# Clustered order for all of batch 2, and batch 3's fetches behind the last block

## The chip, the core and the metric

One NeuronCore of a Trainium2 chip runs the whole program. The time is the device time of one execution in microseconds (us). Five engines work side by side, each in the order of its own queue, and wait for each other by semaphores: TensorE (PE, matmuls; its weight loads are listed as PEld), VectorE (DVE), ScalarE (ACT), GpSimd (POOL), and SyncE (SP), which here only issues DMAs. PE writes to PSUM, the others read it from there.

## The reference

Clustered attention, then a two-layer network, in float32. Every query and key belongs to the cluster whose centroid is nearest in direction, and a query attends to the keys of its own cluster only.

```python
batch, n_heads, seq, head_dim, n_clusters = 4, 8, 768, 64, 16
q_assign = argmax(einsum('bhsd,hcd->bhsc', q_n, c_n))       # k_assign likewise
mask = q_assign[:, :, :, None] == k_assign[:, :, None, :]
scores = where(mask, scale * q @ k.T, -1e9)
attn = softmax(scores) @ v                                   # (4, 8, 768, 64)
x = attn.transpose(0, 2, 1, 3).reshape(3072, 512)
h = x @ w_in                                                 # (3072, 2048)
out = (maximum(h, 0) + alpha * minimum(h, 0)) @ w_out        # (3072, 512)
```

## The kernel before

**Pairs, units, steps.** Work on attention goes by pairs of heads: `pairs` has 16 of them, number n = 4 * batch + pair. A *dense* pair is computed in two halves of 384 queries, each against all six chunks of 128 keys, with everything outside the cluster multiplied by zero (`mask`, L806). A *clustered* pair (n >= `NO` = 10, so 10 and 11 of batch 2 and all of batch 3) has its rows sorted by cluster first; then each chunk of keys needs only the queries of its neighbouring chunks (`window`), 16 blocks of 128 x 128 instead of 36. One half of a dense pair, or one clustered pair, is a unit of three steps u; from step 24 (`TOGETHER`) a unit has 15 ticks: three in which it scores (`score`, L765) and weighs the unit before (`weigh`, `weigh_near`), and twelve slots.

**Filler.** PE's other work is the network on half a batch (`ffn_pieces`): 16 hidden pieces (L1027) and 12 final pieces (L1045), 28 in all. `feeds` says at which step the pieces of which half batch become available, `begun_at` where blocks of steps begin, and the slots of a block take its pieces evenly, down to `kept` pieces that stay for the next. Blocks after step 48 are 48 to 60 (pairs 10, 11, first halves of 8 and 9; pieces of the second half of batch 1), 60 to 66 (second halves of 8 and 9; batch 2, first half) and 66 to 78 (pairs 12 to 15; batch 2, second half). Behind step 78 (`NS`) come the 12 pieces kept, and then `last_pieces`: the network on batch 3 in a form with fewer products (L1205, L1261). `w_in_sums` prepares `w_in` for it and is tied to two of the last kept pieces.

**Sorting a pair.** `ORDERS` gives the step at which a clustered pair's q and k are loaded. `order_features` (DVE transposes) and `order_sims` (PE) follow, then a chain on DVE (`order_counts` to `order_clusters`: argmax, a scan, ranks, the clusters of the sorted places), spread over ticks. `order_rows` then puts the pair's 24 scatters and six stage loads into the deque `sorting`. `order_stage` loads four blocks of rows of q, k and v by three DMAs on SP's queue into one of two stages; `order_scatter` (L663, POOL) writes one block to its sorted places in DRAM by an indirect DMA. In each slot of the main loop the deque is emptied up to one scatter, so 12 a unit. `order_load`, 3 or 4 steps before the pair's first step, reads the sorted rows back (12 DMAs on SP).

**Back to the rows.** In the unit after a clustered pair, `normalise_near` (DVE) writes its outcome, `to_rows` (L964, PE, and a copy on ACT, L967) turns it, and `put_back` (L972, POOL) writes it to its rows by 12 indirect DMAs, one a tick from 8 and from 14 ticks behind `normalise_near`. `fetch_back` (L984) reads it again by four DMAs on SP's queue, 20 ticks behind `normalise_near`, and nine ticks later `turn_back` (L991, DVE) transposes it into `xT`, the network's input. For the last pair these distances are shorter (`dense`).

**Rows sums.** `total` (L856) sums the softmax denominators on PE in the last slot of a unit; `invert` (L869) takes their reciprocals on DVE a few ticks later. `misc()` is a single PSUM buffer that `total`, the second side of `weigh_near`, `to_rows`, `order_sims` and others share in turn.

Of the kernel before, what the change touches and what calls it, by code (L numbers as in the profile page):

```python
# [23 lines left out]
def kernel(  # L24
# [70 lines left out]
    def later(slots, piece):  # L95
        due.setdefault(now[0] + slots, []).append(piece)
# [5 lines left out]


    pairs = [(b, hp) for b in range(B) for hp in range(NCH)]
    NO = WHOLE * NCH - 2
    NP = len(pairs)
    raw_qk, vts = {}, {}

# [383 lines left out]
    def second_part():  # L492

        first_part.close()
        for name, bufs in (("emore", 1), ("ordc", 1), ("ordp", 1), ("order", NP - NO),
                           ("xmore", 1), ("byrow", 1)):
# [148 lines left out]
    def order_stage(n, i):  # L645
# [5 lines left out]
        for src, p0, d0 in ((q, 0, 0), (k, TS, 0), (v, TS, D)):  # L651
            nc.sync.dma_start(out=t[p0:p0 + TS, :, d0:d0 + D],
                              in_=src[b, head, rows].rearrange("(x p) d -> p x d", p=TS))

    def order_scatter(n, i, x):
        h, part = divmod(i, PARTS)
        m = NX // PARTS
        xx = part * m + x
        if x == 0:
            nc.gpsimd.tensor_copy(  # L660
                out=sorts["stage"][i % STAGES].bitcast(I32)[0:TS, :, D],
                in_=sorts["number"][0:TS, part * m:(part + 1) * m])
        nc.gpsimd.indirect_dma_start(  # L663
            out=scratch[n][1][h * NX + xx],
            out_offset=bass.IndirectOffsetOnAxis(ap=ranks[n][:, xx, h:h + 1], axis=0),
            in_=sorts["stage"][i % STAGES][:, x, :], in_offset=None,
            element_offset=h * 2 * S * P)

    def order_load(n):
        whole = scratch.pop(n)[0]  # L670
        found = sorts["order"].tile([P, 2, NJ, 1], I32, name="found")
        for h in range(2):
            r0 = 2 * h * S
            nc.sync.dma_start(out=found[:, h], in_=whole.bitcast(I32)[
                r0:r0 + S, D:D + 1].rearrange("(j p) d -> p j d", p=P))
        orders[n] = found
        for w in range(2):
            raw = inp.tile([P, 2, NJ, D], FP32, name="qk")
            for h in range(2):
                r0 = (2 * h + w) * S  # L680
                for x in range(D // Q):
                    r = h * D + x * Q
# [32 lines left out]
    for b in range(B):  # L715
        whole = [n for n in range(b * NCH, (b + 1) * NCH) if n >= NO]
        rest = [n for n in range(b * NCH, (b + 1) * NCH) if n < NO]
        begun_at.append(len(steps))
        steps += [(n, None, s) for n in whole for s in range(SB)]
        for half in range(2) if rest else ():  # L720
            if half:
                begun_at.append(len(steps))
            steps += [(n, half, s) for n in rest for s in range(SB)]
            feeds[len(steps)] = b, half
    begun_at.append(len(steps))
    assert NJ == 6 and GROUP == 2

# [209 lines left out]
    def normalise_near(n):  # L937
        outT = inp.tile([P, 2, NJ, D], FP32, name="qk").rearrange("p h j d -> p (h j d)")
        for side in range(2):
            nc.vector.tensor_tensor(out=outT[:, side * HS:(side + 1) * HS],  # L940
                                    in0=pos.pop((n, side))[:, 0:HS],
                                    in1=rds.pop((n, side)), op=ALU.mult)
        whole = tc.dram_tile([2 * S, D], FP32, name=f"back{n}")
        to = dram_disjoint_views(whole, 2 * NJ)
        found = orders.pop(n)
        place = found[:, :, :, 0]
        nc.vector.tensor_scalar(out=place, in0=place, scalar1=0, scalar2=S - 1,
                                op0=ALU.max, op1=ALU.min)
        rows = [sorts["byrow"].tile([P, HJ, P], FP32, name=f"rows{i}") for i in range(2)]

        dense = n == NP - 1
        starts = (6, 9) if dense else (6, 12)
        for i in range(2):
            later(starts[i], lambda i=i: to_rows(outT, rows, i))
            for x in range(NJ):
                later(starts[i] + 2 + (x // 2 if dense else x),
                      lambda i=i, x=x: put_back(to, place, rows, i * NJ + x))
        later(starts[1] + 2 + (HJ if dense else NJ), lambda: fetch_back(n, whole))

    def to_rows(outT, rows, i):  # L960

# [12 lines left out]
            out_offset=bass.IndirectOffsetOnAxis(ap=place[:, h, j:j + 1], axis=0),  # L974
            in_=rows[j // HJ][:, j % HJ, h * D:(h + 1) * D], in_offset=None, element_offset=h * S * D)

    def fetch_back(n, whole):

        b, hp = pairs[n]
        raw = inp.tile([P, 2, NJ, D], FP32, name="qk").rearrange("p h j d -> p (h j d)")  # L980
        for h in range(2):
            for x in range(D // Q):
                r = h * D + x * Q
                nc.sync.dma_start(  # L984
                    out=raw[r:r + Q, :].rearrange("p (t i) -> p t i", i=Q),
                    in_=whole[h * S:(h + 1) * S, x * Q:(x + 1) * Q].rearrange(
                        "(t p) i -> p t i", p=Q))

        def turn_back():
            for half in range(2):  # L990
                nc.vector.transpose(out=x_tile(b, half)[:, hp, :],  # L991
                                    in_=raw[:, half * HS:(half + 1) * HS])
        later(4 if n == NP - 1 else 9, turn_back)

    def x_tile(b, half):
        if (b, half) not in xTs:
# [330 lines left out]
    FREE = SLOTS * SB - 3  # L1327


    ORDERS = [26, 30, 34, 38, 41, 51]  # L1330
    prep_at, load_at = {}, {}
    for (n, half), u in start_of.items():
        def at(step, slot, piece):
            prep_at.setdefault((step, slot), []).append(piece)
        if half is None:
            t = ORDERS[n - NO]
            load_at.setdefault(t, []).append(lambda n=n: load(n))
            for i in range(2):
                at(t + 2, 2 + i, lambda n=n, i=i: order_features(n, i))
            at(t + 3, FIRST + 1, lambda n=n: order_sims(n))  # L1340
            load_at.setdefault(u - (3 if n == NO + 1 else 4), []).append(
                lambda n=n: order_load(n))
            at(u - 4, 0, lambda n=n: prep_clusters(n))
            for i in range(2):
                at(u - 1, i, lambda n=n, i=i: order_blocks(n, i))
                at(u - 1, FIRST + i, lambda n=n, i=i: order_queries(n, i))
            continue
# [39 lines left out]
    def feed_block(u):  # L1387
        if u == NS:

            for i, p in ((5, 0), (7, 1)):  # L1390
                ffn[i] = lambda piece=ffn[i], p=p: (piece(), w_in_sums(p))
            ffn.extend(last_pieces())
            return
        ffn.extend(ffn_pieces(*feeds[u]))

    def kept(u):


        return {NS: 12, begun_at[-2]: 8, begun_at[-3]: 2}.get(block_end(u), 0)

    def block_end(u):
        return min(x for x in begun_at if x > u)
# [59 lines left out]
    for u in range(TOGETHER, NS + 1):  # L1462
# [4 lines left out]
        if s == 0 or u == NS:  # L1467
# [2 lines left out]
            tick()  # L1470
            if u < NS:
                score(n, half, range(0, NJ // 2), alone=NJ // 2 - 1)
            tick()
            if prior[1] is None:
                invert(prior[0], 0, 1)
# [22 lines left out]
            if half is None:  # L1498
# [2 lines left out]
                         lambda n=n: (turn(n, 0), rows_sums(n, 0)),  # L1501
                         lambda n=n, E=of: add_near(n, 1, E),
                         lambda n=n: (turn(n, 1), rows_sums(n, 1))]
                todo += [lambda: None] * 4 + [lambda n=n: total(n)]
            else:
                todo.append(lambda E=E: add_up(E[1], E[0]))
                for c in range(2, NJ):
                    todo.append(lambda c=c, E=E: add_up(E[c]))
                todo.append(lambda n=n, half=half: (turn(n, half), rows_sums(n, half)))
                todo += [lambda: None] * 2  # L1510
                todo.append(lambda n=n: total(n))
            slots = range(3, SLOTS)
        else:
            slots = range(SLOTS)
# [2 lines left out]
        for i in slots:  # L1517
# [4 lines left out]
            room = (block_end(u) - block_start(u)) // SB * FREE  # L1522
            pieces = len(ffn) - kept(u) + -whole * (room - 1 - at_slot) // room
            todo.popleft()()
            while sorting:
                scatters, piece = sorting.popleft()
                piece()
                if scatters:
                    break
            feed(max(pieces, 0))  # L1530
            if (s, i) == (SB - 1, SLOTS - 1) and unfinished[0]:
                feed(1)
# [225 lines left out]
```

## Time and profile before

| | |
|---|---|
| median of 4 runs (lowest, highest) | 989.3 us (984.01, 997.01) |
| profiled execution, its own time | 989.48 us |
| its span, first to last instruction | 987.4 us |
| mean granted TensorE clock | 0.986 |
| DMA traffic | 73.35 MB, mean 74 GB/s |
| scatters, L663 on POOL | 144, 157.8 us busy, mean 1095 ns |
| put-backs, L972 on POOL | 72, 76.0 us busy, mean 1056 ns |

The units' first scores stand in PE's timeline at these times (us): step 48 at 454.0, 51 at 479.4, 54 at 525.6, 57 at 563.4, 60 at 594.2, 63 at 639.1, 66 at 682.8, 69 at 710.1, 72 at 736.9, 75 at 765.3; step 78 begins at 791.5, `last_pieces` at 834.75. Busy times in some of these stretches, in us (in brackets the instructions), then the granted clock, the DMA share and GB/s; the columns are the stretch, its length, PE, PEld, DVE, ACT, POOL:

```profile
421.10:454.00 32.90, 32.58 (x117) 15.18 (x116) 26.30 (x45) 5.75 (x11) 10.32 (x12) 1.00 0.31 74
454.00:479.40 25.40, 25.40 (x111) 13.54 (x110) 22.84 (x43) 6.88 (x14) 6.07 (x7) 1.00 0.95 135
479.40:525.60 46.20, 40.52 (x141) 18.79 (x140) 29.04 (x55) 7.75 (x16) 27.76 (x31) 0.93 0.29 66
525.60:563.40 37.80, 25.77 (x115) 13.70 (x114) 20.80 (x36) 7.77 (x15) 16.58 (x17) 0.82 0.17 41
```

How to read the other views: "x4 ... <- ..." is a group of instructions with what it writes and reads; "[0.30 <-issue]" is the idle time of the engine just before and what ended it ("issue": nothing that the profile shows); in a list of waits the three numbers are the total in us, how often, and the longest. In the row of slices each digit is a busy share in tenths of a fortieth of the span, 24.7 us.

### The profile page before, as it was taken

Reading aid. Unit: us, or ns where it says so; the run is one execution under the profiler, and the core shown is the slowest. Engines: PE = TensorE matmul, PEld = TensorE weight load, DVE = VectorE, ACT = ScalarE, POOL = GpSimd, SP = SyncE. Lnnn points to the kernel's source line nnn. Section 1 sums busy time; section 2 is a strip of 40 time slices with the busy share of each in tenths; the row PEclk is TensorE's granted clock in tenths of the full one; section 3 lists DMA queues with packets and bytes.
Section 4 is the critical chain, followed back from the end, with each engine's and each line's share of the span. In section 5 each row is a group of like instructions: output and inputs, shape, how many; then the busy total and the mean of one; then the engine's idle time right before and its main releaser. Section 6 shows DMA issues by size and latency. Waiting matters only on the chain.

```text
span 987.4 us, 11347 instructions
## 1 busy us (share of the span) xinstructions
PE 940.6 (95%) x3995; PEld 502.0 (51%) x3995; DVE 671.9 (68%) x1235; ACT 252.5 (26%) x462; POOL 299.1 (30%) x333
## 2 busy tenths in 40 slices
PE   8999999999999999899895999989999999999997
PEld 5434444454454454444442544545455554556886
DVE  5897789798497786978771875445888536498200
ACT  5664534222131221222111312122122210211000
POOL 1332222110026472431555476550044342000000
PEclk9999999999999999999987999999999999999999
DMA  7442675074004654136712024542031112000000
GB/s 284 126 135 88 141 150 99 16 127 119 0 11 112 155 124 74 44 85 100 134 39 60 25 64 104 97 97 48 22 72 30 30 32 57 1 0 1 21 22 25
DMA packets 209665, 73.35 MB, mean 74 GB/s; under 512 B 194289, under 2 KB 198081, under 8 KB 209601
## 3 DMA queue, kind: packets, MB, share of 16 engines
q1 hardware_dynamic: 201840, 60.35, 28.3%
q0 software_dynamic: 6912, 11.81, 3.6%
q8 instruction: 33, 0.54, 0.2%
q10 hardware_dynamic: 848, 0.39, 0.2%
q14 instruction: 32, 0.25, 0.1%
HBM read 49.89 MB, written 22.28 MB: 73 GB/s over the span
## 4 chain that ended last, share of the span: by engine, by line
PE 80%; DVE 9%; issue 4%; another core or an unknown queue 2%; DMA 1%; ACT 1%; POOL 1%; ACTq 0%; DVEq 0%; SPq 0%; POOLq 0%
PE fps L1045 23%; PE fps L1027 21%; PE sps L765 7%; PE vps L901 7%; PE sps L1261 4%; PE sps L1205 4%; PE fps L765 3%; PE vps L1261 2%; PE vps L1205 2%; PE fps L1261 1%; PE fps L1205 1%; PE mps L934 1%; PE vps L934 1%; POOL back L972 1%
## 5 line engine op out<-in xcount | busy, mean ns | idle before, releaser
L1027 PE MATMUL fps<-xT,w_in_sb 128*128 128x384 f32 x768 | 260.7, 493 | 0.0
L1045 PE MATMUL fps<-w_out_sb,gT 128*128 128x512 f32 x576 | 255.8, 596 | 2.7 <-issue 1.6
L663 POOL DMA_INDIRECT scratch<-stage,off x144 | 157.8, 1095 | 221.0 <-DVE off L619 73.8
L1027 PEld LDWEIGHTS fps<-xT,w_in_sb 128*128 128x128 f32 x768 | 143.2, 191 | 105.0 <-issue 6.7
L1045 PEld LDWEIGHTS fps<-w_out_sb,gT 128*128 128x128 f32 x576 | 107.0, 190 | 130.9 <-issue 122.8
L972 POOL DMA_INDIRECT back<-rows,found x72 | 76.0, 1056 | 141.5 <-ACT rows L967 121.5
L1033 ACT COPY gT<-fps 128x384 f32<-128x384 f32 x96 | 46.0, 479 | 229.7 <-PE fps L1027 209.9
L765 PE MATMUL sps<-qkT 64*128 64x384 f32 (+1 forms) x480 | 93.5, 496 | 2.1 <-issue 1.9
L1019 DVE SCALAR_TENSOR_TENSOR gT<-gT,alpha 128x384 f32<-128x384 f32 x96 | 61.4, 648 | 49.0 <-ACT gT L1033 40.9
L806 DVE SCALAR_TENSOR_TENSOR more<-aq,key,more 128x384 f32<-128x384 bf16 (+1 forms) x120 | 65.2, 599 | 21.8 <-ACT more L786 17.3
L806 DVE SCALAR_TENSOR_TENSOR E<-aq,key,E 128x384 f32<-128x384 bf16 (+1 forms) x96 | 51.8, 594 | 38.9 <-ACT E L786 32.0
L786 ACT ACTIVATE E<-sps 128x768 f32<-128x768 f32 (+1 forms) x78 | 58.4, 796 | 72.0 <-PE sps L774 38.4
L765 PEld LDWEIGHTS sps<-qkT 64*128 64x128 f32 x480 | 45.0, 188 | 44.8 <-issue 18.0
L901 PE MATMUL vps<-E,vt 128*64 128x384 f32 x316 | 58.6, 495 | 1.4 <-DVE xT L1003 1.4
L765 PE MATMUL fps<-qkT 64*128 64x384 f32 x144 | 34.9, 525 | 14.9 <-ACT y L1051 11.4
L271 POOL TENSOR_TENSOR w_in_sb<-w_in_sb,power 128x512 f32<-128x512 f32 x16 | 24.0, 1499 | 70.4 <-DVE w_in_sb L268 70.4
L816 DVE TENSOR_TENSOR acc<-acc,E 128x768 f32<-128x768 f32 x37 | 35.2, 952 | 14.6 <-ACT E L786 13.6
L786 ACT ACTIVATE more<-sps 128x768 f32<-128x768 f32 (+1 forms) x42 | 31.5, 782 | 42.0 <-PE sps L765 26.5
L1051 ACT COPY y<-fps 128x512 f32<-128x512 f32 x18 | 10.6, 586 | 118.7 <-PE fps L1045 72.1
L271 POOL TENSOR_TENSOR w_out_sb<-w_out_sb,power 128x512 f32<-128x512 f32 x16 | 22.9, 1434 | 57.3 <-DVE w_out_sb L268 57.3
L901 PEld LDWEIGHTS vps<-E,vt 128*64 128x64 f32 x316 | 20.1, 136 | 29.2 <-issue 26.5
L1053 DVE TENSOR_TENSOR y<-y,fps 128x512 f32<-128x512 f32 x24 | 16.4, 682 | 24.5 <-PE fps L1045 24.5
(281 smaller groups left out, 1113.5 us busy)
## 6 DMA issues: line engine op xcount, KB each, us to landing
raw<-in_moe_w_in_dram SPq DMA_DIRECT2D x16, 512.0 KB
raw<-in_moe_w_out_dram SPq DMA_DIRECT2D x16, 512.0 KB
out_dram<-y SPq DMA_DIRECT2D x21, 256.0 KB
qk<-in_q_dram SPq DMA_DIRECT2D x48, 96.0 KB
qk<-in_k_dram SPq DMA_DIRECT2D x48, 96.0 KB
qk<-scratch SPq DMA_DIRECT2D x48, 96.0 KB
w_in_kept<-w_in_sb SPq DMA_DIRECT2D x8, 512.0 KB
vt<-in_v_dram SPq DMA_DIRECT2D x10, 384.0 KB
```

The lines of the kernel that those rows point to most:

```text
L271: nc.gpsimd.tensor_tensor(out=dst, in0=dst, in1=power[0].bitcast(FP32), op=ALU.mult)
L663: nc.gpsimd.indirect_dma_start(out=scratch[n][1][h * NX + xx], out_offset=bass.IndirectOffsetOnAxis(ap=ranks[n][:, xx, h:h + 1], axis=0), ...
L765: nc.tensor.matmul(out=bank(ps, h, m), lhsT=qkT[r:r + D, S + c * P:S + (c + 1) * P], rhs=qkT[r:r + D, tokens], start=True, stop=not early_ ...
L786: nc.scalar.activation(out=E[:, :, 0:m], in_=ps[:, :, 0:m], func=AF.Exp, scale=SCALE)
L806: nc.vector.scalar_tensor_tensor(out=e, in0=of, scalar=keys[n][:, NJ + c, h:h + 1], in1=e, op0=ALU.is_equal, op1=ALU.mult)
L901: nc.tensor.matmul(out=po[r:r + D, 0:HS], lhsT=vts[n][:, h, c, :], rhs=e[:, h, :], start=(c == 0), stop=(c == NJ - 1))
L972: nc.gpsimd.indirect_dma_start(out=to[i], out_offset=bass.IndirectOffsetOnAxis(ap=place[:, h, j:j + 1], axis=0), in_=rows[j // HJ][:, j % ...
L1019: nc.vector.scalar_tensor_tensor(out=gs[f], in0=gs[f], scalar=alpha[:, f:f + 1], in1=gs[f], op0=ALU.mult, op1=ALU.max)
L1027: nc.tensor.matmul(out=ps[:, 0:HS], lhsT=w_in_sb[:, c, f * P:(f + 1) * P], rhs=xTs[b, half][:, c, :], start=(c == 0), stop=(c == NCH - 1))
L1045: nc.tensor.matmul(out=ps[:, 0:DM], lhsT=gs[f][:, i * P:(i + 1) * P], rhs=w_out_sb[:, f, :], start=on and f == f0, stop=off and f == f0 + ...
L1205: nc.tensor.matmul(out=bank[to], lhsT=w_in_form(m, x, cc), rhs=rhs[:, cc, :], start=start and cc == 0, stop=cc == KH - 1, skip_group_check ...
L1261: nc.tensor.matmul(out=bank[to], lhsT=g_form(m, x, t), rhs=w_out_form(n, x), start=start and x == 0, stop=x == NQ - 1, skip_group_check=no ...
```

## The change

- `NO` becomes 8: all four pairs of batch 2 are clustered. The steps of batch 2 and 3 are then 48 to 72, eight units of one pair each; `NS` is 72.
- The blocks behind step 48 become 48 to 66 (pairs 8 to 13) with the pieces of batch 1's second half, and 66 to 72 (pairs 14, 15) with the pieces of both halves of batch 2. `kept` leaves 34 pieces behind step 72, and 2 behind steps 48 and 66.
- `ORDERS` has eight entries, every third step; features and similarities come one step earlier after the load. A unit's slots take up to 17 scatters: two in both slots of its first step and in three others.
- For batch 3 `fetch_back` no longer follows each pair: all four fetches are queued behind the last block, at ticks 1, 4, 7 and 14 behind the last `normalise_near`. `turn_back` follows its fetch by 7 ticks instead of 9 (4 for the last pair, as before).
- `total` moves from a unit's last slot to behind the first scores of the next unit.
- `order_load` comes three steps ahead for all but the first clustered pair.

```diff
-    NO = WHOLE * NCH - 2
+    NO = (WHOLE - 1) * NCH
...
+        if b < WHOLE:
+            begun_at.append(len(steps))
+        else:
+            begun_at.append(len(steps) + 2 * SB)
+            feeds[len(steps) + 2 * SB] = [(b - 1, 0), (b - 1, 1)]
         steps += [(n, None, s) for n in whole for s in range(SB)]
...
-        later(starts[1] + 2 + (HJ if dense else NJ), lambda: fetch_back(n, whole))
+        backs[n] = whole
+        if pairs[n][0] < B - 1:
+            later(starts[1] + 2 + NJ, lambda: fetch_back(n))
+        elif dense:
+            for i in range(NCH):
+                later((1, 4, 7, starts[1] + 2 + HJ)[i],
+                      lambda i=i: fetch_back(NP - NCH + i))
...
-        later(4 if n == NP - 1 else 9, turn_back)
+        later(4 if n == NP - 1 else 7, turn_back)
...
-    ORDERS = [26, 30, 34, 38, 41, 51]
+    ORDERS = [26, 29, 32, 35, 38, 41, 44, 47]
...
-                at(t + 2, 2 + i, lambda n=n, i=i: order_features(n, i))
-            at(t + 3, FIRST + 1, lambda n=n: order_sims(n))
-            load_at.setdefault(u - (3 if n == NO + 1 else 4), []).append(
+                at(t + 1, FIRST + i, lambda n=n, i=i: order_features(n, i))
+            at(t + 2, 2, lambda n=n: order_sims(n))
+            load_at.setdefault(u - (3 if n > NO else 4), []).append(
                 lambda n=n: order_load(n))
...
-            for i, p in ((5, 0), (7, 1)):
+            for i, p in ((-7, 0), (-5, 1)):
...
-        return {NS: 12, begun_at[-2]: 8, begun_at[-3]: 2}.get(block_end(u), 0)
+        return {NS: 34, begun_at[-2]: 2, begun_at[-3]: 2}.get(block_end(u), 0)
...
                 score(n, half, range(0, NJ // 2), alone=NJ // 2 - 1)
+            total(prior[0])
             tick()
...
-                todo += [lambda: None] * 4 + [lambda n=n: total(n)]
+                todo += [lambda: None] * 5
...
-            while sorting:
+            room = 1 + (s == 0 or (s, i) in ((1, 0), (1, 3), (2, 1)))
+            while sorting and room:
                 scatters, piece = sorting.popleft()
                 piece()
-                if scatters:
-                    break
+                room -= scatters
```

More of the change, by code (lines that the diff above doesn't have):

```diff
@@ L494, in second_part @@
         first_part.close()
-        for name, bufs in (("emore", 1), ("ordc", 1), ("ordp", 1), ("order", NP - NO),
+        for name, bufs in (("emore", 1), ("ordc", 1), ("ordp", 1), ("order", 6),
                            ("xmore", 1), ("byrow", 1)):
@@ L653, in order_stage @@
                               in_=src[b, head, rows].rearrange("(x p) d -> p x d", p=TS))
+    scattered = {}
     def order_scatter(n, i, x):
+        scattered.setdefault(n, []).append((i, x))
         h, part = divmod(i, PARTS)
@@ L669, in order_load @@
     def order_load(n):
+        assert len(scattered[n]) == 2 * NX
         whole = scratch.pop(n)[0]
@@ L717 @@
         rest = [n for n in range(b * NCH, (b + 1) * NCH) if n < NO]
-        begun_at.append(len(steps))
+        if b < WHOLE:
[3 more added lines that the diff above has]
+            feeds[len(steps) + 2 * SB] = [(b - 1, 0), (b - 1, 1)]
         steps += [(n, None, s) for n in whole for s in range(SB)]
@@ L723 @@
             steps += [(n, half, s) for n in rest for s in range(SB)]
-            feeds[len(steps)] = b, half
+            feeds[len(steps)] = [(b, half)]
     begun_at.append(len(steps))
@@ L957, in normalise_near @@
                       lambda i=i, x=x: put_back(to, place, rows, i * NJ + x))
-        later(starts[1] + 2 + (HJ if dense else NJ), lambda: fetch_back(n, whole))
+        backs[n] = whole
[5 more added lines that the diff above has]
+                      lambda i=i: fetch_back(NP - NCH + i))
+    backs = {}
     def to_rows(outT, rows, i):
@@ L975, in put_back, with fetch_back @@
             in_=rows[j // HJ][:, j % HJ, h * D:(h + 1) * D], in_offset=None, element_offset=h * S * D)
-    def fetch_back(n, whole):
+    def fetch_back(n):
         b, hp = pairs[n]
+        whole = backs[n]
         raw = inp.tile([P, 2, NJ, D], FP32, name="qk").rearrange("p h j d -> p (h j d)")
@@ L1393, in feed_block @@
             return
-        ffn.extend(ffn_pieces(*feeds[u]))
+        for b, half in feeds[u]:
+            ffn.extend(ffn_pieces(b, half))
     def kept(u):
-        return {NS: 12, begun_at[-2]: 8, begun_at[-3]: 2}.get(block_end(u), 0)
+        return {NS: 34, begun_at[-2]: 2, begun_at[-3]: 2}.get(block_end(u), 0)
     def block_end(u):
@@ L1509 @@
                 todo.append(lambda n=n, half=half: (turn(n, half), rows_sums(n, half)))
-                todo += [lambda: None] * 2
-                todo.append(lambda n=n: total(n))
+                todo += [lambda: None] * 3
             slots = range(3, SLOTS)
@@ L1521 @@
             at_slot = (u - block_start(u)) // SB * FREE + (s * SLOTS + i - 3)
-            room = (block_end(u) - block_start(u)) // SB * FREE
-            pieces = len(ffn) - kept(u) + -whole * (room - 1 - at_slot) // room
+            places = (block_end(u) - block_start(u)) // SB * FREE
+            pieces = len(ffn) - kept(u) + -whole * (places - 1 - at_slot) // places
             todo.popleft()()
-            while sorting:
+            room = 1 + (s == 0 or (s, i) in ((1, 0), (1, 3), (2, 1)))
+            while sorting and room:
                 scatters, piece = sorting.popleft()
                 piece()
-                if scatters:
-                    break
+                room -= scatters
             feed(max(pieces, 0))
```

## The prediction

> **What bounds the kernel now.** I read, in order: the page's busy table, the chain of work that ended last, the list of what TensorE (PE) waited for, PE's timeline by unit, and the timelines of POOL and SP.
>
> The span is 987.4 us, the profiled execution's own time 989.48 us, so 2.1 us lie around the span; the median of the four runs is 989.3 (984.0 to 997.0). The sum below is made against 987.4.
>
> ```profile
> span 987.4 us, 11347 instructions
> PE 940.6 (95%) x3995; PEld 502.0 (51%) x3995; DVE 671.9 (68%) x1235; ACT 252.5 (26%) x462; POOL 299.1 (30%) x333
> ...
> POOL 1332222110026472431555476550044342000000
> ...
> PE fps L765 <- ACT y L1051: 11.4, 1, 11.4
> SPq L984 <- DMA back<-rows,found: 37.8, 6, 20.6
> ```
>
> PE is busy 95% of the span, so removed PE work should pay. POOL's 30% is an average: it is idle in the last quarter and at 4 to 7 tenths between 300 and 670 us, where scatters and put-backs fall. The last line is SP's queue, held at fetch_back until a pair's put-backs had landed, once for 20.6 us.
>
> Price of attention on PE, first a dense half (steps 57 on), then a clustered pair (69 on):
>
> ```profile
> 563.35 1.56 PE L765 MATMUL sps<-qkT 64*128 64x384 f32 x8
> ...
> 566.02 2.16 PE L901 MATMUL vps<-E,vt 128*64 128x384 f32 x12
> 568.00 2.10 PE L901 MATMUL vps<-more,vt 128*64 128x384 f32 x12
> ...
> 572.17 8.01 PE L1027 MATMUL fps<-xT,w_in_sb 128*128 128x384 f32 x24
> ```
>
> ```profile
> 710.12 1.35 PE L765 MATMUL sps<-qkT 64*128 64x256 f32 x8
> ...
> 717.57 2.84 PE L1045 MATMUL fps<-w_out_sb,gT 128*128 128x512 f32 x6
> ```
>
> From first score to first FFN matmul: 8.8 us for a dense half (0.5 of it a neighbour's L598), so 8.3, and 16.6 for a dense pair; 7.45 for a clustered pair, plus two groups of transposes of 0.33, so 8.1.
>
> POOL's price, beside a nearly idle DVE:
>
> ```profile
> 505.60 0.95 POOL L663 DMA_INDIRECT scratch<-stage,off  x1 [0.30 <-issue]
> 506.86 0.96 POOL L972 DMA_INDIRECT back<-rows,found  x1 [0.30 <-issue]
> ...
> 513.09 0.20 POOL L660 COPY stage<-number 64x4 int32<-64x4 int32 x1
> 513.57 0.98 POOL L663 DMA_INDIRECT scratch<-stage,off  x1 [0.28 <-issue]
> ...
> 531.96 3.53 SPq L984 DMA_DIRECT2D qk<-back  x4
> ```
>
> Start to start is 1.265 us; a copy adds 0.48 to every fourth scatter, so 1.38 for a scatter, 1.265 for a put-back. Pair 10's put-backs end at 529.9, its fetch is issued from 531.96, its landings run to 538.3: 9.4 us from the last put-back's start to data.
>
> **The change, part by part.** A unit is three steps, 15 ticks.
>
> *Pairs 8 and 9 clustered.* PE loses 2 x (16.6 - 8.1) = 17 us, all on the bound engine. An FFN hidden piece costs 2.65 us, a final one 3.52; their number (84 from step 48 on) is unchanged. POOL gains 48 scatters and 24 put-backs: 48 x 1.38 + 24 x 1.265 = 97 us. SP gains some 34 DMAs a pair (18 stage loads at 0.61, 12 of order_load, 4 of fetch_back), 20 us a pair: hidden, SP's own issue time being far below a unit, except where they stand behind a wait (rival 3).
>
> *Where the FFN goes.* Steps 48 to 66 are now six clustered units with 28 pieces (16 hidden, 12 final: 84.6 us); with 6 x 8.1 = 48.6 and 1 for order_sims that is 134 us, 22.3 a unit. Steps 66 to 72 are two units with 24 pieces: 70.6 + 16.2 = 87. Behind them lie 34 pieces (16 hidden, 18 final: 105.8) and the last pair's weigh_near and transposes (4.2): 110. The last product stays at 152.65.
>
> *Seventeen scatters a unit.* Eight pairs make 192 scatters. The first ranks come at about step 31.5 (load 26, features 27, sims 28, then some 17 ticks); 192/17 = 11.3 units end at about step 65.4, just before pair 15's order_load at 66. So half of them, 96, still stand in POOL's queue at step 48, and from step 51 each unit adds the 12 put-backs of the pair before. That is 17 x 1.38 + 12 x 1.265 = 38.6 us of POOL in a unit with 22.3 us of PE. Under a working DVE it is more: from 552.5 to 588.8 POOL made 25 indirect DMAs and 3 copies in 36.3 us while DVE was busy 93%; at the idle rate they are 33.1. I take +5% for a DVE that is busy for somewhat over half of such a unit, 40.5, and add 2 because SP issues the next stage's loads behind the fetch it holds: 42.5. Bounds: 38.6 and 44.5.
>
> The Trainium skill ("SBUF — State Buffer", section "A bandwidth-pool intuition that's wrong (but worth ruling out)") says that GpSimd's descriptor writing is locked out for as long as some DVE operations hold the shared port, 620 ns becoming about 3100. The rows show 0.95 at least, 1.095 on average and 4.24 once. An estimate by that page with every operation blocked would be some 90 us a unit; the measured 10% decides, and the sum does not use it.
>
> *Who waits.* Pair 8's put-backs are queued from tick 10 of unit 51, SP's fetch at tick 7 of unit 54, and DVE's turn_back at tick 14. PE reaches that tick 27 us after tick 10. POOL needs 12 put-backs and 13 scatters, 33.1 x 1.05 = 35, then 9.4 to landing: 44. So DVE stands at turn_back for some 17 us with masks, slopes, reciprocals and the next transposes queued behind; PE goes on for about 5 us (a score group, a few pieces), then lacks `invert` and the free misc bank. From there each turn_back (pairs 9, 10, 11) comes one POOL unit after the one before. Steps 48 to 66: 36.7 to the first put-back, 44.4, 3 x 42.5 = 127.5, 3 to the block's end, less PE's 5 ahead: 207 us, where PE alone needs 134.
>
> *Batch 3's fetches behind the last block.* For pairs 12 to 14 that moves 12 DMAs (0.52 us each on SP) and 6 transposes (0.55 each on DVE), 6.2 and 3.3 us, from units with spare time on both engines into the tail, and takes SP's waits for put-backs out of the last block. In the tail pair 15's 12 put-backs start about 12 us in, take 15, land 9 later: DVE stands at its turn_back until about 36 us. The cover is the pieces: finals first, then eight hidden ones that need only ACT, about 42 us. Nothing lost; without the cover about 10 us. In units 66 and 69 (43.5 us each) POOL has only the put-backs, and pair 15's load lands some 16 us after step 66, needed at 29: nothing.
>
> *`total` behind the first score.* PE stood before L856 for 0.73, 1.33, 0.73 and 1.28 us between 225 and 454; the score (1.9 us) covers that: -4 there. Later ones vanish in POOL's pace.
>
> *Orders every three steps.* DVE's order chain is about 10.2 us a pair (transposes, argmax, scan, ranks, clusters, from their rows). Between 198 and 454 DVE was busy 205 us; about two more chains and pair 8's preparation make 226 of 256. PE gains 2 us of sims and begins; for DVE's crowding I take 1 (bounds 0 and 10). Two finals move behind step 48: -7. Step 48 then begins at 454 - 4 + 3 - 7 = 446.
>
> *At nothing:* the moved w_in_sums (same pieces), wider `begins`, loads at u - 3 instead of u - 4 (off the path while POOL is late), `order` kept at six buffers.
>
> **Sum.** 446 + 207 + 87 + 110 + 152.65 = 1003, plus 2.1: **1005 us**. The 17 us of PE, the 4 us, and the before's own losses in that stretch (11.4 at 527.8, 3.6 at 645.3, about 10 of slow issue near 488 and 640) disappear under 73 us of waiting for POOL. With the bounds (POOL unit 38.6 to 44.5, crowding 0 to 10, a returning stall up to 15) my likeliest case spans 990 to 1030.
>
> **Rivals.**
> 1. *POOL keeps up, faster.* Scatters run so far ahead in the dense units (17 x 1.38 = 23.5 us in units of about 32) that few are left at step 51. Then 446 + 134 + 87 + 110 + 153 = 930, with up to 25 us of stalls as now: 932 to 957, about 945. For it: 25% spare POOL time before 48. Against: the stage loads stand in SP's queue behind output stores and order loads, and POOL idled 68.4 us on `stage` in before. It decides if 29 operations fit in 22.3 us, 0.77 each; the smallest seen is 1.26. 13%.
> 2. *Late but less, within 1%.* One unit's scatters are ahead at step 51 (-23) or POOL runs at 38.6 (-12): 982 to 993. 25%.
> 3. *SP makes it worse.* While SP stands at fetch_back the output stores and stage loads behind it stand too, and POOL starves; before, POOL paused from 535.2 to 552.5 after such a fetch. Another 5 to 10 us in each of four units: 1025 to 1045. 12%.
> 4. The likeliest, as summed: 50%. That scatters miss their load is excluded by the count, 65.4 before 66.
>
> **Numbers.** About 1% (979 to 999) is what a measurement of this kernel tells from no change. Faster: rival 1 and a little of 2, 0.14; same 0.24; slower 0.62. The range for 8 in 10, 968 to 1028, leaves out rival 1 and the worst of rival 3.
>
> **What would show it.** Right: between steps 51 and 66 the POOL row near its top with 0.30 us between operations, units about 42 us apart, DVE's longest waits at L991's transposes for the fetch, PE gaps of 10 to 18 us there with a lower granted clock; no gap in the tail. Wrong: six units of 22 to 25 us, POOL waiting for `rows` or `stage` rather than being waited for; or large DVE-made gaps before step 48.

## The result and the profile after

The changed kernel takes 1092.5 us (median of 10 runs, 1078.6 to 1100.55) against 989.7 (15 runs, 972.9 to 1004.57): a ratio of 1.108, 95% interval 1.1005 to 1.1149. It is slower, as forecast, but by 103 us where 16 were forecast, and outside the range. The profiled execution took 1088.75 us, 1086.8 of them its span, at a mean granted clock of 0.938 (0.986 before).

The page of the changed kernel, its busy table and three rows of slices, each 27.2 us long:

```profile
span 1086.8 us, 11472 instructions
...
PE 952.6 (88%) x3931; PEld 511.1 (47%) x3931; DVE 657.6 (61%) x1229; ACT 246.1 (23%) x450; POOL 359.3 (33%) x417
...
PE   8999999999997899796718355779999999999997
...
POOL 3232222100557771507665563752413200000000
PEclk9999999999998899899869686779999999999999
```

PE has 64 matmuls fewer than before, yet its busy time has risen by 12 us, because some ran at a lower clock. The holes in its row (7, 1, 8, 3, 5, 5, 7) lie where POOL's row, there mostly indirect DMAs, is at 3 to 7 and not at its top.

The prediction expected DVE to stand at the transposes of fetch_back, by then L1008. DVE's and ACT's lists of waits in the changed kernel (total, how often, longest) say otherwise:

```profile
DVE qk L948 <- remote: 52.5, 5, 20.5
...
DVE inverses L877 <- remote: 27.1, 4, 18.7
...
DVE xT L1008 <- DMA qk<-back: 2.7, 1, 2.7
```

```profile
ACT more L791 <- remote: 99.7, 10, 30.6
ACT E L791 <- remote: 24.1, 4, 13.9
```

The predicted wait is 2.7 us. In its place stand waits that end with "remote": a releaser that the profile cannot name, as nothing on this core ended just then. Before, the largest such wait was one of 20.3 us, ACT's at L1051. To see what they are, here is the longest one: PE's, ACT's and POOL's timelines around 547 to 572 us, one fence each.

```profile
546.78 0.37 PE L773 MATMUL sps<-qkT 64*128 64x256 f32 x1 [0.22 <-issue]
572.04 1.65 PE L1044 MATMUL fps<-xT,w_in_sb 128*128 128x384 f32 x2 [24.89 <-ACT more L791]
```

```profile
540.08 0.87 ACT L791 ACTIVATE E<-fps 128x384 f32<-128x384 f32 x2 [0.39 <-issue]
571.50 0.87 ACT L791 ACTIVATE more<-fps 128x384 f32<-128x384 f32 x2 [30.55 <-remote]
```

```profile
565.18 0.96 POOL L666 DMA_INDIRECT scratch<-stage,off  x1 [0.30 <-issue]
566.45 0.95 POOL L666 DMA_INDIRECT scratch<-stage,off  x1 [0.30 <-issue]
```

PE had finished its scores by 547.2. ACT, which needs nothing but those scores, took them at 571.5. In between PE did nothing, and DVE had one instruction of 0.56 us; only POOL worked, as the windows of that stretch show (start and end, length, then busy time and count of PE, PEld, DVE, ACT, POOL; granted clock, DMA share, GB/s):

```profile
536.30:547.20 10.90, 10.63 (x58) 5.73 (x58) 7.08 (x15) 2.28 (x4) 8.33 (x10) 0.76 0.23 62
547.20:572.00 24.80, 0.00 (x0) 0.00 (x0) 1.10 (x3) 0.50 (x2) 15.68 (x18) 0.59 0.62 117
```

By the modelled ends of the matmuls the results were there and did not arrive. POOL had put out indirect DMAs, some 1.27 us apart, from 525.5 to 567.4, and the results came through together 5 us after its last one had begun. I counted this over whole traces: for every ACT or DVE instruction that waited for a result of PE, the time from that matmul's modelled end to the semaphore event that released it. (In this kernel only these two engines read what PE writes.) It is usually 0.01 to 0.05 us. Over 1 us, called late from here on, were 11 of 274 before (32 us together) and 41 of 287 in the changed kernel (200 us, the longest 24.4). Such counts shift by about a tenth with the rule for which waits to take in: a second rule gives 11 of 279 (32 us) and 44 of 294 (216 us). 27 of the 41 came while indirect DMAs had filled over 0.6 of POOL's last 6 us, most of the others within 5 us behind the last DMA of such a burst. Results of ACT and DVE are not held: in the same traces they arrive within 13 ns.

### The profile page after: what moved, and what is told of

Same layout as the page of the kernel before. It is cut to its first block, busy times and chain, and to the rows that moved or that the text cites. A ratio compares the mean times of both kernels' runs of the same rounds, so it can differ in the third digit from the quotient of the medians.

```text
span 1086.8 us, 11472 instructions
## 1 busy us (share of the span) xinstructions
PE 952.6 (88%) x3931; PEld 511.1 (47%) x3931; DVE 657.6 (61%) x1229; ACT 246.1 (23%) x450; POOL 359.3 (33%) x417
## 4 chain that ended last, share of the span: by engine, by line
PE 76%; DVE 10%; another core or an unknown queue 8%; issue 5%; ACT 1%; DVEq 0%; POOL 0%; POOLq 0%; ACTq 0%
PE fps L1044 22%; PE fps L1062 21%; PE sps L773 6%; PE vps L909 4%; PE sps L1278 4%; PE sps L1222 4%; PE fps L773 2%; PE vps L1278 2%; PE vps L1222 2%; PE mps L942 2%; PE vps L942 1%; PE fps L1278 1%; PE fps L1222 1%; DVE E L814 1%
## 5 line engine op out<-in xcount | busy, mean ns | idle before, releaser
L1044 PE MATMUL fps<-xT,w_in_sb 128*128 128x384 f32 x768 | 272.7, 511 | 42.3 <-ACT more L791 31.8
L666 POOL DMA_INDIRECT scratch<-stage,off x192 | 197.0, 1026 | 204.0 <-DVE acc L824 63.6
L1044 PEld LDWEIGHTS fps<-xT,w_in_sb 128*128 128x128 f32 x768 | 149.5, 199 | 153.0 <-ACT more L791 34.4
L988 POOL DMA_INDIRECT back<-rows,found x96 | 93.6, 975 | 131.3 <-ACT rows L983 74.6
L773 PEld LDWEIGHTS sps<-qkT 64*128 64x128 f32 x448 | 45.2, 197 | 60.7 <-issue 27.2
L877 DVE RECIPROCAL inverses<-mps 64x12 f32<-64x12 f32 (+1 forms) x40 | 10.3, 258 | 90.4 <-PE mps L864 34.6
L814 DVE SCALAR_TENSOR_TENSOR more<-aq,key,more 128x384 f32<-128x384 bf16 (+1 forms) x110 | 58.6, 588 | 3.7 <-ACT more L794 2.2
L909 PE MATMUL vps<-E,vt 128*64 128x384 f32 x272 | 50.7, 496 | 1.4 <-DVE xT L1020 1.4
L791 ACT ACTIVATE more<-fps 128x384 f32<-128x384 f32 x34 | 15.7, 492 | 128.7 <-remote 99.7
L814 DVE SCALAR_TENSOR_TENSOR E<-aq,key,E 128x384 f32<-128x384 bf16 (+1 forms) x82 | 43.4, 580 | 1.2 <-ACT E L794 1.0
L271 POOL TENSOR_TENSOR w_out_sb<-w_out_sb,power 128x512 f32<-128x512 f32 x16 | 22.9, 1432 | 57.3 <-DVE w_out_sb L268 57.3
L824 DVE TENSOR_TENSOR acc<-acc,E 128x768 f32<-128x768 f32 x30 | 28.6, 952 | 14.5 <-ACT E L794 13.6
```

Of the source, the lines that this page charges most:

```text
L271: nc.gpsimd.tensor_tensor(out=dst, in0=dst, in1=power[0].bitcast(FP32), op=ALU.mult)
L666: nc.gpsimd.indirect_dma_start(out=scratch[n][1][h * NX + xx], out_offset=bass.IndirectOffsetOnAxis(ap=ranks[n][:, xx, h:h + 1], axis=0), ...
L773: nc.tensor.matmul(out=bank(ps, h, m), lhsT=qkT[r:r + D, S + c * P:S + (c + 1) * P], rhs=qkT[r:r + D, tokens], start=True, stop=not early_ ...
L814: nc.vector.scalar_tensor_tensor(out=e, in0=of, scalar=keys[n][:, NJ + c, h:h + 1], in1=e, op0=ALU.is_equal, op1=ALU.mult)
L909: nc.tensor.matmul(out=po[r:r + D, 0:HS], lhsT=vts[n][:, h, c, :], rhs=e[:, h, :], start=(c == 0), stop=(c == NJ - 1))
L988: nc.gpsimd.indirect_dma_start(out=to[i], out_offset=bass.IndirectOffsetOnAxis(ap=place[:, h, j:j + 1], axis=0), in_=rows[j // HJ][:, j % ...
```

## The experiments

**First question: which part of the change is it?** Four theories. QUEUE is the prediction's: POOL's queue is too long and others wait for what it delivers. SIGNAL: PE's results come late while POOL issues indirect DMAs back to back. TRAFFIC: the bytes and packets of the added transfers slow everything. REST: the change's other parts (orders, schedule, fetches).

`e1_no_indirect`: in the changed kernel both kinds of indirect DMA become plain ones on the queues of SP and ACT. The sort by cluster and its undoing are left out. `e2_plain_back` does so for the put-backs alone, `e3_plain_scatter` for the scatters alone.

```diff
-        nc.gpsimd.indirect_dma_start(out=scratch[n][1][h * NX + xx], ...)
+        if x == m - 1:
+            for w in range(2):
+                r = (2 * h + w) * S + part * m * TS
+                nc.sync.dma_start(out=scratch[n][0][r:r + m * TS, :]..., in_=sorts["stage"][i % STAGES][w * TS:(w + 1) * TS, :, :])
...
-        nc.gpsimd.indirect_dma_start(out=to[i], ...)
+        if j % HJ == HJ - 1:
+            nc.scalar.dma_start(out=whole[h * S + (j - HJ + 1) * P:h * S + (j + 1) * P, :]..., in_=rows[j // HJ][:, :, h * D:(h + 1) * D])
```

> The changed kernel with POOL's indirect DMAs taken out: each stage goes to the scratch rows in plain order by two DMAs on SP's queue, each put-back by plain DMAs on ACT's queue, four a pair. The rows are not sorted and not put back, so the attention of pairs 8 to 15 is over the wrong neighbours; PE, DVE and ACT do the same work. Theory QUEUE (the prediction's: POOL's backlog makes the fetches late, DVE stands at turn_back): 935 to 960 us. Theory SIGNAL (while POOL issues indirect DMAs one after another, results of PE reach ACT and DVE many us late, and PE stands): 935 to 960 us too, and no PE result over 1 us late. Theory TRAFFIC (order_load, fetch and stage loads in small pieces on SP hold PE up, POOL is innocent): above 1060 us, since these stay. Theory REST (the moved total, the 34 pieces, the late fetches): above 1060 us.

> The changed kernel with the put-backs alone as plain DMAs on ACT's queue (rows stay in sorted order, so the outcome of pairs 8 to 15 stands at wrong rows); the 192 scatters stay. QUEUE: POOL has 23.5 us a unit against 22 to 25 of PE, the backlog is gone: 940 to 960 us. SIGNAL: POOL is still issuing 17 scatters a unit nearly without a pause in steps 48 to 66, so PE stands still now and then, less than with put-backs: 985 to 1050 us. TRAFFIC and REST: above 1060 us.

> The changed kernel with the scatters alone as plain DMAs on SP's queue, two a stage (rows unsorted, so the attention of pairs 8 to 15 is over the wrong neighbours); the 12 put-backs a pair stay indirect. QUEUE: 935 to 960 us. SIGNAL: bursts of at most 12 operations with pauses between them, 15 us of POOL a unit: 940 to 975 us. TRAFFIC and REST: above 1060 us.

`e4_before_17`: the kernel before with nothing of the change but its 17 scatters a unit.

```diff
-            while sorting:
+            room = 1 + (s == 0 or (s, i) in ((1, 0), (1, 3), (2, 1)))
+            while sorting and room:
                 scatters, piece = sorting.popleft()
                 piece()
-                if scatters:
-                    break
+                room -= scatters
```

> The kernel before with one part of the change alone: up to 17 scatters a unit instead of 12, the six clustered pairs as they were. The number of POOL operations is the same, they come closer together. QUEUE: they are done earlier, so 980 to 992 us, not slower. SIGNAL: longer unbroken bursts, PE results late more often, 1000 to 1030 us. TRAFFIC: no change, 985 to 993. REST: no change.

Measured: e1 964.9 us (ratio to before 0.974, 0.969 to 0.979), no late result among 275; e2 997 in two executions and 1012 in the other two, 19 late, 71 us together; e3 970.2 (0.980, 0.974 to 0.985), 8 late, 22 us; e4 1002.0 (1.011, 1.005 to 1.017), 13 late, 47 us. TRAFFIC and REST fall: the same bytes in the changed schedule run faster than before once POOL does not issue them. SIGNAL has the times of e2, e3 and e4, and e1's lack of late results; e1's time is 5 us above what it and QUEUE gave. QUEUE misses e2 by 37 us or more and e3 and e4 by 10. But these four don't say that POOL's queue costs nothing, only that late results cost something.

**Second question: what of POOL's work holds results up?** `e5_pool_plain` keeps every DMA where it stands on POOL, but in the plain form; `e6_pool_compute` is e1 with four small copies on POOL, into a spare tile `pad`, in each of the places.

```diff
-        nc.gpsimd.indirect_dma_start(out=scratch[n][1][h * NX + xx], ...)
+        r = (h * NX + xx) * P
+        nc.gpsimd.dma_start(out=scratch[n][0][r:r + P, :], in_=sorts["stage"][i % STAGES][:, x, :])
...
-        nc.gpsimd.indirect_dma_start(out=to[i], ...)
+        nc.gpsimd.dma_start(out=whole[h * S + j * P:h * S + (j + 1) * P, :], in_=rows[j // HJ][:, j % HJ, h * D:(h + 1) * D])
```

```diff
+        for _ in range(4):
+            nc.gpsimd.tensor_copy(out=sorts["pad"], in_=sorts["number"][0:TS, 0:4])
```

> The changed kernel with each of its 288 indirect DMAs (192 scatters, 96 put-backs) replaced by one plain DMA of the same 128 rows of 512 bytes, still issued by POOL in the same place of its queue; rows are then left in token order, so the sort and its undoing are left out. INDIRECT (TensorE's results are held up by the indirect form alone, in which POOL handles every row's address): 955 to 985 us, as with no DMA on POOL at all (964.9), and fewer than 5 results over 1 us late. ISSUE (any DMA that POOL issues in close order holds them up): 1020 to 1095 us, and 20 or more late results.

> The changed kernel with its indirect DMAs replaced by plain ones of SP and ACT (the sort is left out, as in the run that took 964.9 us), and in each of the 288 places of POOL's queue four small copies of 64x4, some 1.1 us by the row of such a copy (0.26 to 0.28 us). INDIRECT and ISSUE: POOL's being busy is harmless, 955 to 985 us, fewer than 5 results over 1 us late. BUSY (it is enough that POOL is busy almost without pause, whatever it does): 1020 to 1095 us, 20 or more late results.

Measured: e5 948.0 us (0.962, 0.955 to 0.970), e6 974.2 (0.989, 0.981 to 0.997); no late result in either (273 waits each). e5 is 7 us faster than INDIRECT gave. POOL's DMA queue moved the same in the changed kernel and in e5 (packets, MB, share of the 16 DMA engines' time):

```profile
q0 software_dynamic: 9216, 15.75, 4.4%
```

```profile
q0 software_dynamic: 9216, 15.75, 4.8%
```

(A row has 512 bytes in a scatter and 256 in a put-back; the expectation gives 512 for both.) So it is the indirect form. What of it, POOL's way of issuing it or the scattered rows that it writes, no run separates. A plain DMA also takes POOL a shorter time, which e5's timeline of POOL shows (0.54 us, against 0.96 and a pause of 0.30):

```profile
568.42 0.54 POOL L985 DMA_DIRECT2D back<-rows  x1
568.95 0.54 POOL L667 DMA_DIRECT2D scratch<-stage  x1
569.48 0.54 POOL L985 DMA_DIRECT2D back<-rows  x1
```

That is why e5 alone cannot acquit POOL's queue.

**Third question: does a pause let results through?** Behind every indirect DMA POOL gets one, two or three copies of 64x4, or one memset of 128x8; nothing is left out of the computation.

```diff
         nc.gpsimd.indirect_dma_start(...)
+        for _ in range(2):
+            nc.gpsimd.tensor_copy(out=sorts["pad"], in_=sorts["number"][0:TS, 0:4])
```

> The changed kernel with two copies of 64x4 on POOL (some 0.55 us) behind every indirect DMA; all 288 stay and nothing is left out. In a burst POOL's share in indirect DMAs falls from 0.77 to about 0.53. SHARE (results are late only where indirect DMAs fill more than about 0.64 of POOL's time): few late results, under 15 over 1 us, and 985 to 1040 us, since POOL's work grows by 155 us and its bursts get longer. COUNT (every indirect DMA holds results up by its own amount, pause or not): 1080 to 1130 us, 35 or more late results.

> The kernel before with three copies of 64x4 on POOL (some 0.8 us) behind every indirect DMA; nothing is left out. POOL's share in indirect DMAs in a burst falls to about 0.46. SHARE: fewer than 4 results over 1 us late (11 in the kernel before) and 965 to 985 us, faster than before. COUNT: as many late results as before, and 988 to 1005 us.

> The changed kernel with one copy of 64x4 on POOL behind every indirect DMA; nothing is left out. By the run with two copies (0.98 + 0.43 + 0.15 us from one indirect DMA to the next in a burst, against 1.265 in the changed kernel, and not one late result) one copy should give about 1.34 us, 22 us of POOL's time in all over 288. LATE (the late results are nearly all of the change's loss): none over 1 us late, 960 to 990 us. BACKLOG (with results on time POOL's 29 a unit bind instead, as the prediction had it): none late, 995 to 1060 us, and DVE's wait at the transposes of fetch_back (74 us with two copies, 2.7 in the changed kernel) is over 20 us. COUNT2 (two copies were enough only because they made the pause long): 20 or more late results, 1060 to 1100 us.

> The changed kernel with one memset of 128x8 on POOL behind every indirect DMA, in which POOL's period stays at 1.27 to 1.30 us. If it is another instruction of POOL between two indirect DMAs that lets results through, none is late and the time is that of the run with one copy or up to 20 us less; if it is the length of the pause, 20 or more are late and the time is 1060 to 1100 us.

> The kernel before with one copy of 64x4 on POOL behind every indirect DMA; nothing is left out. LATE: no late results (11 before, of 32 us together, among them a gap of 11.4 us in TensorE's row), 968 to 984 us. BACKLOG: none late, but 985 to 1000 us as with three copies (994.5).

> The kernel before with two copies of 64x4 on POOL behind every indirect DMA, 1.57 us from one to the next in a burst; nothing is left out. By the runs with one copy (969.4 us, 7 late results of 18.5 us together) and three (994.5, none late): none late, and 965 to 980 us if POOL still keeps up at this pace, 980 to 992 if its backlog already binds.

| kernel | median start to start of indirect DMAs, us | late results: number, sum | time, us | ratio to before (95%) |
|---|---|---|---|---|
| after | 1.264 | 41, 200 us | 1092.5 | 1.108 (1.101 to 1.115) |
| e10, after and a memset | 1.271 | 33, 179 us | 1093.4 | 1.096 (1.090 to 1.103) |
| e9, after and one copy | 1.353 | 19, 81 us | 1046.4 | 1.048 (1.041 to 1.055) |
| e7, after and two copies | 1.576 | 0 | 1092.5 | 1.109 (1.100 to 1.118) |
| before | 1.268 | 11, 32 us | 989.7 | 1 |
| e11, before and one copy | 1.351 | 7, 18.5 us | 969.4 | 0.976 (0.968 to 0.983) |
| e14, before and two copies | 1.698 | 0 | 972.9 | 0.981 (0.976 to 0.986) |
| e8, before and three copies | 1.984 | 0 | 994.5 | 1.007 (1.004 to 1.011) |

(The medians are of DMAs that start less than 2.5 us apart.) The pace does it, or the pause that grows with it, not that another instruction stands between: the memset, which leaves the pace as it was, changes little. Late results vanish by 1.58 us. But e7, with none of them, is no faster than the changed kernel: SHARE was right on the late results and wrong on the time. In e8 it was so too (no late result, but 994.5 us and not 965 to 985). e7's lists of waits show what took their place, first DVE's, then ACT's:

```profile
DVE xT L1013 <- DMA qk<-back: 74.0, 5, 21.3
...
DVE qkT L706 <- DMA qk<-scratch: 52.2, 9, 13.6
```

```profile
ACT rows L986 <- DMA back<-rows,found: 124.2, 8, 21.8
```

This is the prediction's own mechanism: everyone waits for put-backs and scatters that POOL has not reached. It is real at 1.58 us a DMA. e9 has both, in part: DVE's wait at those transposes was 31.1 us and its time is in BACKLOG's range, but 19 results were still late, so none of its three theories had all its numbers. e11 is as fast as LATE said with 7 still late; and e8's 47.1 us at the same transposes show the backlog in the kernel before, too.

**Fourth question: does the backlog bind at the changed kernel's own pace?** Plain DMAs on POOL as in e5, with two and three copies behind each: POOL is as much taken up, and no result is late.

> The changed kernel with its 288 indirect DMAs replaced by plain ones on POOL (the sort and its undoing are left out), and two copies of 64x4 behind each: 0.54 us for a plain one (it took that in the run of 948.0 us, where no result was late), 0.43 for two copies and 0.15 to 0.3 between, so POOL is taken up for 1.12 to 1.27 us a DMA, near the 1.265 of the changed kernel, without its late results. LATE: the pace alone costs little, 950 to 975 us. BACKLOG (the prediction's mechanism: 29 a unit at this pace are too many): 985 to 1040 us, with DVE at the transposes of fetch_back over 15 us.

> The changed kernel with its 288 indirect DMAs replaced by plain ones on POOL (the sort and its undoing are left out), and three copies of 64x4 behind each instead of the two of the run of 988.6 us: by the steps there (0.54 us a DMA, 0.2 to 0.25 a copy) 1.2 to 1.3 us a DMA, the changed kernel's own 1.265. BACKLOG (POOL's pace binds by itself, and the more the slower): no late results, and 1000 to 1040 us, on the line between 988.6 (two copies) and 1092.5 (indirect DMAs with two copies, 1.57 us); the prediction's 1005 belongs to this case. If the pace had already done its harm with two copies, the time stays within 8 us of 988.6, and the late results alone make up the 100 us that the changed kernel takes more.

Measured: e13 988.6 us (0.9995, 0.996 to 1.003) at a median of 1.03 us a DMA; e15 1026.0 (1.039, 1.029 to 1.050) at 1.268, the changed kernel's pace. No late result in either. BACKLOG holds (DVE's wait at the transposes of fetch_back is 36.1 us in e13); the time grows from e5's 948 at 0.53 us. e15's waits, DVE's and ACT's:

```profile
DVE xT L1009 <- DMA qk<-back: 51.2, 5, 16.1
...
DVE qkT L704 <- DMA qk<-scratch: 31.1, 6, 11.0
```

```profile
ACT rows L983 <- DMA back<-rows: 71.1, 7, 14.0
```

The first scores of the units tell where the two losses lie (us, from PE's timelines of the profiled executions):

| | step 48 | 51 | 54 | 57 | 60 | 63 | 66 | 69 | span |
|---|---|---|---|---|---|---|---|---|---|
| e5: plain, 0.53 us | 445.9 | 473.0 | 501.5 | 528.2 | 549.8 | 572.1 | 598.0 | 642.5 | 946.9 |
| e15: plain, 1.268 us | 446.0 | 473.1 | 501.7 | 537.8 | 577.9 | 621.5 | 668.1 | 719.0 | 1023.5 |
| after: indirect, 1.264 us | 473.3 | 500.4 | 536.3 | 591.1 | 636.9 | 687.9 | 737.7 | 782.3 | 1086.8 |

From e5 to e15 (POOL's pace alone) 77 us are lost, all behind step 54. From e15 to after (the indirect form, at the same pace) 63 us are lost: 27 before step 48, 42 between 48 and 66, and 6 come back behind. A plain DMA also lands sooner, but by little: its last packet ends 1.5 us after POOL's instruction began in e15 (median), an indirect one's 1.95 us in the changed kernel. An estimate from these: with two such landings to wait for in each of six units, 6 of the 63 us. For the rest the trace shows the late results, 200 us of which a part lies beside other work.

**The move of total by itself** was tried on e11:

```diff
                 score(n, half, range(0, NJ // 2), alone=NJ // 2 - 1)
+            total(prior[0])
             tick()
...
-                todo += [lambda: None] * 4 + [lambda n=n: total(n)]
+                todo += [lambda: None] * 5
```

> The same kernel with the change's move of total as well (behind the first score instead of at the end of the steps' list). By the prediction that part alone takes 4 to 8 us away; if the move is worth nothing without the rest, the time is within 3 us of the run without it.

Measured: 969.75 us (0.973, 0.966 to 0.980) against 969.4 without it. Step 48 begins 3.2 us earlier (450.1 against 453.3), near the forecast 4 there, but step 66 does not (664.6 against 664.0). The gain is lost again between steps 60 and 66 (578.1 against 582.0 at step 60), so the second expectation held; that POOL's pace takes it there is likely, but not shown.

e11 is faster than both kernels and leaves nothing out. PE's row and clock in its page:

```profile
PE   8999999999999999999997999999999999999997
...
PEclk9999999999999999999999899999999999999999
```

## Why the prediction was right or wrong

- **The step that failed is "Who waits".** It took each wait for a wait on what POOL delivers, and had no term for results of PE that are held up while POOL issues indirect DMAs. At the transposes of fetch_back DVE waited 2.7 us, not 17 and then a unit at a time. PE and its consumers stood instead in "remote" waits, and being late themselves they gave POOL time to catch up: between steps 48 and 66 it was busy for 156.8 of 264.4 us, and itself waited 22.9 us for ACT's `rows`, which the prediction had named as a sign of being wrong.
- **That mechanism was right where results are on time.** In e15 the sum can be laid beside the trace: step 48 at 446.0 (forecast 446), three units of 40.1, 43.6 and 46.6 us from step 57 (forecast 42.5), steps 48 to 66 in 222.1 (forecast 207), DVE at fetch_back up to 16.1 us (forecast 17). ACT's wait for `rows` to be free, 71.1 us, stood beside these and had not been named. Its 1026 lies in the range, 21 above the number. The remaining 63 us are, but for the few of landing, the missing term.
- **The sign was in the profile of before.** The prediction quotes PE's gap of 11.4 us before L765, released by ACT's y L1051, and counts it among losses that POOL's pace would swallow. Followed one step further, to ACT's timeline of the kernel before, that instruction had itself waited 20 us, with no releaser that the profile can name:

```profile
538.56 0.59 ACT L1051 COPY y<-fps 128x512 f32<-128x512 f32 x1 [20.28 <-remote]
```

  PE had run nothing since 527.8; POOL's burst had its last indirect DMA at 534.2. One long case and ten short ones in the kernel before became 41 in the changed one, where 72 more indirect DMAs come and the room of 17 packs them closer: that room alone costs 1.1% in e4.
- **The count of POOL's work was right, two readings were not.** Scatters took 1026 ns on average (197.0 us over 192), put-backs 975; 96 scatters were issued before step 48, as forecast, and the last at 725.9, before the last load at step 66 (737.7). But from 552.5 to 588.8 the kernel before made 23 indirect DMAs and 3 copies, not 25 and 3, so beside the working DVE they took 19% more than at the idle rate, not 10%; half of that gives 44 us a unit for the sum's 42.5, still within its bounds. And POOL's row of before has digits from 1 to 7, not 4 to 7, between 300 and 670 us, and begins its last quarter with 4, 3, 4 and 2; the sum uses neither. The rule of the Trainium skill that the prediction weighed ("SBUF — State Buffer", "A bandwidth-pool intuition that's wrong (but worth ruling out)"), GpSimd locked out by DVE, shows no more here than before. What hurt runs the other way: while POOL issued, what DVE and ACT wait for came late.
- **PE's price of 134 us for steps 48 to 66** was too low even without POOL: e5 takes 152.1 there, with PE busy for 141.9 of them at a clock of 0.97 and DVE for 142.6, so neither alone can be called the bound. Rival 1 had allowed up to 25 us for stalls, and its 932 to 957 is the size of a kernel whose POOL keeps up, e5's 948; with indirect DMAs POOL does not.
- **The clock** added to it, as forecast for gaps of 10 to 18 us. In the stretch of 24.8 us above it was granted at 0.59, while PE did nothing: it fell to half 4.5 us after the last matmul. The Trainium skill ("TensorE: Matmul & The Clock Gate", "What's actually happening") puts the array at half rate after an idle window of about 3.4 us; the stretches at half clock in these traces, but for one at each kernel's end, last 3.4 us or a multiple of it, which agrees.
- **Right as summed:** step 66 to the last product in 196 us (forecast 87 + 110), the last product in 153 (152.65), and no gap over 0.9 us in the tail. Step 48 of e15 came where the sum of the three small terms before it had put it, which does not show each of them. Rival 2 fell. Rival 3 had the right size (1025 to 1045) for e15, by another way than SP. The pause of POOL that it quotes, 535.2 to 552.5, ended with ACT's `rows` L967 and not with a load; it follows the stand of PE and ACT that is shown above.

## What to carry to other kernels

Where a wait of ACT or DVE ends with a releaser that the profile cannot name, look up whether the matmul it needs had long ended, and what POOL was doing meanwhile. If POOL was issuing indirect DMAs back to back, space them: one small copy behind each made the kernel before 2.4% faster, two took all late results away, and three cost more than they saved. Count POOL's time per unit first, since the spacing must fit beside what the unit's other engines do.

## What the runs showed of the hardware

- While POOL issued indirect DMAs of 128 rows (of 512 or 256 bytes) 1.26 us apart, and up to 5 us behind the last of them, results of PE reached ACT and DVE up to 24.4 us after the matmul's modelled end, against 0.01 to 0.05 us as a rule; at 1.35 us apart fewer were late, at 1.58 and more none (0 of 253 in e7, 275 in e14, 276 in e8).
- Plain DMAs from POOL 0.53 us apart, or copies on POOL almost without pause, held up none (0 of 273 each); nor did plain DMAs with copies behind them at 1.268 us, the changed kernel's pace (e15). Results of ACT and DVE were not held in any of these traces (13 ns at most).
- An indirect DMA kept POOL busy for 0.96 us and a pause of 0.30, a plain one for 0.54. The first packet moved 1.55 us after POOL's instruction began (median) in the changed kernel, 1.1 us in e15.
- Why is open. The ends of matmuls are modelled, so the trace does not tell for sure whether the matmul's true end or only its signal was late. The clock's fall to half 4.5 us after the last matmul's modelled end, as where PE stands idle, speaks for the signal. No run here looked inside POOL.
